# Attention with one query: loads of eight heads at 64 KiB per partition in three buffers, with V loaded one place behind K

## The chip, the cores and the metric

The kernel runs on one NeuronCore of a Trainium2 chip; the other cores of the chip are idle. The metric is the time of one execution on the device in microseconds, lower is better. The span of a profile, from the first to the last instruction, is about 1.7 us shorter than the time of the same execution (before: 1260.5 against 1262.21 us).

## The reference

```python
B, H, Sq, Skv, Dh = 8, 32, 1, 4096, 128        # bfloat16
def reference(q, k, v):
    scale = q.shape[-1] ** -0.5
    scores = jnp.einsum('bhqd,bhkd->bhqk', q, k) * scale
    attn = softmax(scores, axis=-1)
    return jnp.einsum('bhqk,bhkd->bhqd', attn, v)
```

There are 256 heads with one query each. Every K and V element is used once: 536.9 MB must be read, and little is computed with each byte.

## The kernel before

A tile is the K (or V) of G = 4 heads: 128 partitions, 32 of them for each head, C = 128 positions in each partition, 128 values per position, 32 KiB per partition, 4 MiB in one load. Five such buffers are shared by K and V. For each tile VectorE (DVE) multiplies K by the query and adds the upper half of the products to the lower (`product`); TensorE (PE) sums the remaining 64 values with an identity matrix into PSUM (`sum_over_d`); DVE finishes the sums and finds one maximum per head (`weights_of`); ScalarE (ACT) takes the exponentials, one pass per head, into a weights tile `w`; PE multiplies weights and V (`values_of`), and a last small product picks each head's own block (`result_of`). `norm_of` sums the exponentials on PE and takes the reciprocal on DVE: this is the normaliser. The last few positions of the last V are multiplied straight into the result, in small matmuls at the very end (the "late" matmuls).

```python
G = 4
SLOTS = 5
R = 4
LAST = 8
# [cut: constants, pools, the query, product, sum_over_d]

    def weights_of(t):
        # [cut: scores from PSUM, maximum, bias per head]
        w = w_pool.tile([P, C, G], BF16, name="w", tag="w")
        # [cut]
        for g in range(G):
            nc.scalar.activation(
                out=w[:, :, g], in_=sc[:], func=ACT.Exp, bias=bias[:, g : g + 1], scale=scale,
                accum_out=esum[:, t % R, g : g + 1],
            )

    def values_of(t, lo, hi):
        # [cut]
        for c0 in range(lo, hi, CB):                     # CB = 4 positions per matmul
            nc.tensor.matmul(
                avs[t][:], lhsT=w[:, c0 : c0 + CB, :], rhs=vt[:, c0 : c0 + CB, :],
                start=(c0 == 0), stop=(c0 + CB == (C if t < NT - 1 else C - LAST)),
            )

    # [cut]
    for t in range(NT - 1):                              # NT = 64
        if t + 2 < NT:
            load("k", t + 2)
        load("v", t)
        # [cut]
        product(t, 0, C // 2)
        if t > 0:
            weights_of(t - 1)
        product(t, C // 2, C)
        if t > 1:
            values_of(t - 2, 0, C)
            result_of(t - 2)
            # [cut: norm_of]
        sum_over_d(t)
    load("v", NT - 1)
    with tc.manual_schedule():
        product(NT - 1, 0, C // 2)
        weights_of(NT - 2)
        product(NT - 1, C // 2, C)
        values_of(NT - 3, 0, C)
        result_of(NT - 3)
        sum_over_d(NT - 1)
        values_of(NT - 2, 0, C // 2)
        weights_of(NT - 1)
        values_of(NT - 2, C // 2, C)
        result_of(NT - 2)
        norm_of(NQ - 1)
        values_of(NT - 1, 0, C - LAST)
        result_of(NT - 1)
```

## Time and profile before

| | before |
|---|---|
| time, median of 3 | 1262.19 us (1262.17 to 1262.36) |
| span of the profile | 1260.5 us |
| DMA between 20 and 1200 us | share 1.00, 431 GB/s |
| last data packet ends | 1254.4 us |
| from there to the end of the span | 6.1 us |

The page of the profile, in parts: the load queue with bytes and its share of the 16 DMA engines; the chain of work that ended last; the exponentials (count, busy time, mean time of one); and the loads, with their number, size and median time from issue to landing.

```profile
q1 hardware_dynamic: 20160, 536.88, 99.2%
...
DMA 67%; PE 24%; DVE 7%; ACT 1%; issue 0%; SPq 0%; ACTq 0%; DVEq 0%
...
L203 ACT ACTIVATE w<-sc,bias 128x128 bf16<-128x128 f32 x256 | 110.9, 567 | 734.0 <-DVE bias L195 734.0
...
kt<-in_k_dram SPq DMA_DIRECT2D x63, 4096.0 KB, 35.2
vt<-in_v_dram SPq DMA_DIRECT2D x61, 4096.0 KB, 29.6
```

The loads take 99.2% of the DMA engines' time and 67% of the chain, so they are what bounds the kernel. A 4 MiB load needs 9.7 us at 431 GB/s, but 29.6 to 35.2 us pass from its issue to its landing: by these medians two other loads were queued ahead of it, so a buffer that comes free a little late costs nothing.

The windows view of before shows each stretch of time with its length, the busy time and number of instructions of PE, weight loads, DVE, ACT and POOL, the granted TensorE clock (1 is full), the DMA share and the rate.

```profile
core 0: us, PE busy (x) PEld busy (x) DVE busy (x) ACT busy (x) POOL busy (x), PEclk, DMA share, GB/s
20.00:1200.00 1180.00, 795.08 (x3193) 297.45 (x3193) 901.54 (x812) 151.22 (x567) 0.00 (x0) 0.83 1.00 431
...
1245.00:1250.00 5.00, 4.33 (x26) 1.78 (x24) 0.33 (x2) 0.77 (x3) 0.00 (x0) 1.00 0.83 340
1250.00:1255.00 5.00, 5.00 (x25) 2.10 (x24) 0.00 (x0) 0.00 (x0) 0.00 (x0) 1.00 0.31 123
```

The DMA is saturated until about 1245 us and runs out between 1245 and 1255 us. The kernel's end is therefore two things: when the last data land, and how much work is still to be done then.

The timeline of before, cut to the end of the kernel. The columns are start, duration, engine, line, operation, output and inputs, count, and in brackets the idle time before it with what ended it.

```profile
1215.84 0.13 PEld L219 LDWEIGHTS <-w 128*16 128x16 bf16 x1 [0.29 <-issue]
1216.26 0.13 PEld L219 LDWEIGHTS <-w 128*16 128x16 bf16 x1 [0.29 <-issue]
...
1241.44 7.07 PE L219 MATMUL av<-vt,w 128*16 128x512 bf16 x32
...
1243.45 0.58 ACT L203 ACTIVATE w<-sc,bias 128x128 bf16<-128x128 f32 x1 [5.94 <-DVE bias L195]
...
1243.85 0.56 ACT L203 ACTIVATE w<-sc,bias 128x128 bf16<-128x128 f32 x1
...
1249.56 6.63 PE L219 MATMUL av<-vt,w 128*16 128x512 bf16 x30
...
1256.23 0.59 ACT L240 ACTIVATE comb<-av 16x512 bf16<-16x512 f32 x1 [7.09 <-PE av L219]
...
1258.22 0.33 ACTq L265 DMA_DIRECT2D out_dram<-stage  x1
```

Weight loads stand 0.42 us apart at the start of a burst of matmuls, while the 32 and the 30 matmuls (7.07 and 6.63 us) run at 0.22 us each: PE is slow at first and then twice as fast. And the exponentials of 128 columns start 0.40 us apart (0.385 us between the next ones). After the last V matmul the rest (copy, combining, late matmuls, store) takes about 4.3 us.

The length of single DMA packets is in the trace's packet records, not on the page. For the load queue of before (bytes, number, median and mean ns):

```
32768  15872  1216   1219.0
16384    256   611.5  613.3
 8192   1408   313    313.7
    4   2240     9      9.1    (semaphore of each load, one per engine)
```

A straight line through the means of these sizes has about 27 GB/s per engine and a fixed part of about 9 ns per packet.

### The profile page before, as it was taken

To read this page: it belongs to the slowest core of one execution; us is meant where nothing else is said; L and a number is where in the kernel's file an instruction comes from. 1 tells how busy PE (TensorE), PEld (TensorE's weight loads), DVE (VectorE), ACT (ScalarE), POOL (GpSimd) and SP (SyncE) were. 2 spreads that over 40 slices of the span, in tenths; PEclk is the share of its full clock that TensorE was granted. 3 is DMA by queue.
4 is the path that set the end of the run, shared out by engine and by line. 5 is a ranking of instruction groups with operands and counts; after the bars stand their busy time and mean duration, and the time that the engine had idled before them with its cause. 6 is when DMAs were issued, how large, how long until landed. Compare 5 with 4: busy or idle time off the path is not lost.

```text
span 1260.5 us, 8779 instructions
## 1 busy us (share of the span) xinstructions
PE 845.2 (67%) x3430; PEld 317.2 (25%) x3430; DVE 940.4 (75%) x851; ACT 164.3 (13%) x609; POOL 2.9 (0%) x14
## 2 busy tenths in 40 slices
PE   1666766856757667677676675766767667667578
PEld 0222222322222222222232222222222222222223
DVE  5869978687686777877778768677686777876873
ACT  0101111111101111011111110110101101111011
POOL 0000000000000000000000000000000000000000
PEclk9778878888789788887787888888888788887889
DMA  9999999999999999999999999999999999999996
GB/s 400 432 431 431 430 433 430 430 430 430 432 432 430 429 433 432 432 433 431 431 432 433 428 432 432 432 429 430 432 431 430 433 432 432 430 431 431 429 424 287
DMA packets 20569, 537.57 MB, mean 426 GB/s; under 512 B 2592, under 2 KB 2592, under 8 KB 2992
## 3 DMA queue, kind: packets, MB, share of 16 engines
q1 hardware_dynamic: 20160, 536.88, 99.2%
q8 instruction: 27, 0.44, 0.1%
q10 hardware_dynamic: 368, 0.13, 0.0%
q14 instruction: 14, 0.11, 0.0%
HBM read 536.94 MB, written 0.07 MB: 426 GB/s over the span
## 4 chain that ended last, share of the span: by engine, by line
DMA 67%; PE 24%; DVE 7%; ACT 1%; issue 0%; SPq 0%; ACTq 0%; DVEq 0%
DMA vt<-in_v_dram 66%; PE av L219 22%; DVE kt L150 4%; DVE kt L153 2%; PE ps L167 2%; DMA kt<-in_k_dram 1%; ACT w L203 0%; DVE sc L180 0%; PE op L244 0%; ACT comb L240 0%; DVE pmax L184 0%; SPq L124 0%; DVE bias L195 0%; DVE spread L186 0%; DVE nmax L191 0%
## 5 line engine op out<-in xcount | busy, mean ns | idle before, releaser
L219 PE MATMUL av<-vt,w 128*16 128x512 bf16 x2046 | 571.9, 449 | 344.1 <-DMA vt<-in_v_dram 344.1
L150 DVE TENSOR_TENSOR kt<-kt,qb 128x4096 bf16<-128x4096 bf16 x256 | 579.1, 2283 | 214.7 <-DMA kt<-in_k_dram 214.7
L219 PEld LDWEIGHTS <-w 128*16 128x16 bf16 x2046 | 207.6, 102 | 704.3 <-issue 537.3
L153 DVE TENSOR_TENSOR kt<-kt 128x2048 bf16<-128x2048 bf16 x256 | 305.7, 1215 | 0.1
L167 PE MATMUL ps<-kt,ident 128*128 128x512 bf16 x1024 | 253.2, 390 | 32.4 <-DVE kt L153 32.4
L203 ACT ACTIVATE w<-sc,bias 128x128 bf16<-128x128 f32 x256 | 110.9, 567 | 734.0 <-DVE bias L195 734.0
L167 PEld LDWEIGHTS <-ident 128*128 128x128 bf16 x1024 | 90.7, 98 | 161.3 <-issue 61.1
L203 ACT ACTIVATION_READ_ACCUMULATOR w<-sc,bias 128x1 f32 x256 | 64.8, 253 | 0.0
L180 DVE TENSOR_REDUCE sc<-ps 128x128 f32<-128x512 f32 x64 | 43.7, 683 | 24.6 <-PE ps L167 24.6
L240 ACT ACTIVATE comb<-av 16x512 bf16<-16x512 f32 x64 | 37.6, 588 | 167.8 <-PE av L219 132.2
L235 DVE RECIPROCAL rz<-zp 16x1 f32<-16x1 f32 x16 | 2.5, 155 | 66.9 <-PE zp L230 66.9
L141 ACT ACTIVATE qb<-qp 128x512 bf16<-128x512 f32 x16 | 9.6, 597 | 179.6 <-DVE kt L150 174.0
L244 PE MATMUL op<-comb,pick 16*16 16x128 bf16 x256 | 25.0, 217 | 6.4 <-ACT comb L240 6.4
L244 PEld LDWEIGHTS <-pick 16*16 16x16 bf16 x256 | 13.7, 84 | 34.2 <-issue 34.2
L135 PE MATMUL qp<-q_all,ident 16*32 16x512 bf16 x64 | 7.6, 430 | 21.6 <-ACT qb L141 14.9
L184 DVE TENSOR_REDUCE pmax<-sc 128x1 f32<-128x128 f32 x64 | 17.7, 277 | 0.1
L186 DVE TENSOR_SCALAR spread<-zero,pmax 128x32 f32<-128x32 f32 x64 | 14.9, 233 | 0.1
L195 DVE TENSOR_SCALAR bias<-own,nmax 128x4 f32<-128x4 f32 x64 | 14.3, 223 | 0.1
L191 DVE TRANSPOSE_TENSOR_REDUCE nmax<-spread 128x1 f32<-128x32 f32 x64 | 13.0, 202 | 0.1
L135 PEld LDWEIGHTS <-ident 16*32 16x32 bf16 x64 | 1.8, 89 | 28.4 <-issue 26.8
L230 PE MATMUL zp<-ones,esum 128*16 128x1 f32 x32 | 3.1, 166 | 8.1 <-ACT w L203 8.1
L259 ACT ACTIVATE stage<-op,rz 16x128 bf16<-16x128 f32 x16 | 5.7, 358 | 11.3 <-PE op L244 10.3
(21 smaller groups left out, 9.0 us busy)
## 6 DMA issues: line engine op xcount, KB each, us to landing
kt<-in_k_dram SPq DMA_DIRECT2D x63, 4096.0 KB, 35.2
vt<-in_v_dram SPq DMA_DIRECT2D x61, 4096.0 KB, 29.6
vt<-in_v_dram SPq DMA_DIRECT2D x11, 1024.0 KB, 22.3
kt<-in_k_dram SPq DMA_DIRECT2D x2, 2048.0 KB, 33.5
vt<-in_v_dram SPq DMA_DIRECT2D x1, 512.0 KB, 18.5
vt<-in_v_dram SPq DMA_DIRECT2D x2, 256.0 KB, 15.8
q_all<-in_q_dram ACTq DMA_DIRECT2D x1, 64.0 KB, 5.9
out_dram<-stage ACTq DMA_DIRECT2D x3, 16.0 KB, 9.9
```

The lines of the kernel that those rows point to most:

```text
L150: nc.vector.tensor_tensor(out=part, in0=part, in1=qb[:, j : j + 1, :].to_broadcast([P, MC, D]), op=ALU.mult)
L153: nc.vector.tensor_tensor(out=part[:, :, 0 : D // 2], in0=part[:, :, 0 : D // 2], in1=part[:, :, D // 2 : D], op=ALU.add,)
L167: nc.tensor.matmul(ps[:], lhsT=ident[:], rhs=kt[:, u * UC : (u + 1) * UC, s * DS : (s + 1) * DS], start=(s == 0), stop=(s == n - 1),)
L180: nc.vector.tensor_reduce(out=sc[:, u * UC : (u + 1) * UC], in_=ps[:], axis=AX.X, op=ALU.add)
L184: nc.vector.tensor_reduce(out=pmax[:], in_=sc[:], axis=AX.X, op=ALU.max)
L186: nc.vector.tensor_scalar(out=spread[:], in0=zero[:], scalar1=pmax[:, 0:1], scalar2=-scale, op0=ALU.add, op1=ALU.mult,)
L191: nc.vector.tensor_reduce(out=nmax[:], in_=spread[:], axis=AX.X, op=ALU.min, apply_transpose=True)
L195: nc.vector.tensor_scalar(out=bias[:], in0=own[:], scalar1=nmax[:, 0:1], scalar2=None, op0=ALU.add)
L203: nc.scalar.activation(out=w[:, :, g], in_=sc[:], func=ACT.Exp, bias=bias[:, g : g + 1], scale=scale, accum_out=esum[:, t % R, g : g + 1],)
L219: nc.tensor.matmul(avs[t][:], lhsT=w[:, c0 : c0 + CB, :], rhs=vt[:, c0 : c0 + CB, :], start=(c0 == 0), stop=(c0 + CB == (C if t < NT - 1 e ...
L240: nc.scalar.activation(out=comb[:], in_=avs.pop(t)[:], func=ACT.Copy)
L244: nc.tensor.matmul(ops[n][:], lhsT=pick[:, m, r, :], rhs=comb[:, m * D : (m + 1) * D], start=(r == 0 and m == 0), stop=(r == R - 1 and m = ...
```

## The change

The tile doubles to eight heads: 64 KiB per partition, 8 MiB per load, with three buffers in place of five. There are half as many loads and packets of, perhaps, twice the size. With only three buffers, each has to be emptied in time, so the schedule is written out by hand and fine-grained: scores in quarters of a tile, each V loaded one place behind its K, and its matmuls spread over the products of two tiles. The first and last loads are cut, and the last tile's exponentials come in two halves, to shorten both ends.

The diff, cut to its core:

```diff
-G = 4
-SLOTS = 5
-R = 4
+G = 8
+SLOTS = 3
+R = 2
-LAST = 8
+LAST = 16
-    UC = 128
+    UC = 64
[cut: pools, query, constants]
     cuts = {
-        ("k", NT - 1): [C // 2] * 2,
-        ("v", NT - 3): [C // 4] * 4,
+        ("k", 0): [C // 4] * 4,
+        ("k", NT - 4): [C // 2] * 2,
+        ("k", NT - 3): [C // 2] * 2,
+        ("k", NT - 2): [C // 2] * 2,
+        ("k", NT - 1): [C // 4] * 4,
         ("v", NT - 2): [C // 4] * 4,
-        ("v", NT - 1): [C // 4] * 3 + [C // 8, C // 16, LAST],
+        ("v", NT - 1): [C // 8] * 7 + [C // 16, LAST],
     }
[cut: q_prep per tile; sum_over_d and scores_of per quarter]
-        for g in range(G):
-            nc.scalar.activation(
-                out=w[:, :, g], in_=sc[:], func=ACT.Exp, bias=bias[:, g : g + 1], scale=scale,
-                accum_out=esum[:, t % R, g : g + 1],
-            )
+        n = C // 2 if t == NT - 1 else C
+        for c0 in range(0, C, n):
+            if c0 > 0:
+                esum = late
+            for g in range(G):
+                nc.scalar.activation(
+                    out=w[:, c0 : c0 + n, g], in_=sc[:, c0 : c0 + n], func=ACT.Exp,
+                    bias=bias[:, g : g + 1], scale=scale, accum_out=esum[:, t % R, g : g + 1],
+                )
[cut: the loop of before and its end]
+    with tc.manual_schedule():
+        q_prep(0)
+        for t in range(NT):                     # NT is now 32
+            if t + 1 < NT:
+                load("k", t + 1)
+            load("v", t)
+            product(t, 0, Q)                    # Q = C // 4
+            if t > 1:
+                values_of(t - 2, 3 * Q, 3 * Q + Q // 2)
+            sum_over_d(t, 0)
+            if t > 1:
+                values_of(t - 2, 3 * Q + Q // 2, C)
+                copy_of(t - 2)
+            if t + 1 < NT:
+                q_prep(t + 1)
+            product(t, Q, 2 * Q)
+            sum_over_d(t, 1)
+            scores_of(t, 0)
+            if t > 1:
+                if t % R == 1:
+                    norm_of(t // R - 1)
+                result_of(t - 2)
+            if t > 0:
+                values_of(t - 1, 0, Q)
+            product(t, 2 * Q, 3 * Q)
+            sum_over_d(t, 2)
+            scores_of(t, 1)
+            if t > 0:
+                values_of(t - 1, Q, 2 * Q)
+            product(t, 3 * Q, C)
+            sum_over_d(t, 3)
+            scores_of(t, 2)
+            scores_of(t, 3)
+            weights_of(t)
+            if t > 0:
+                values_of(t - 1, 2 * Q, 3 * Q)
+        values_of(NT - 2, 3 * Q, C)
+        copy_of(NT - 2)
+        norm_of(NQ - 1)
+        result_of(NT - 2)
+        values_of(NT - 1, 0, C - LAST)
+        copy_of(NT - 1)
+        result_of(NT - 1)
```

More of the change, by code (lines that the diff above doesn't have):

```diff
@@ L40 @@
     scale = float(D) ** -0.5
-    UC = 128
+    UC = 64
     DS = 512 // UC
     NU = C // UC
-    MC = 32
+    MC = UC
     CB = 4
@@ L47 @@
     NQ = NT // R
-    assert NQ <= P and C % CB == 0
-    q_n = q.rearrange("b h o d -> (b h o d)").rearrange("(n x) -> n x", n=NQ)
+    TB = 32
+    assert NH % P == 0 and P % G == 0 and TB % PH == 0 and C % CB == 0
+    q_n = q.rearrange("b h o d -> (b h o) d").rearrange("(x p) d -> p x d", p=P)
     o_n = out.rearrange("b h o d -> (b h o) d").rearrange("(n u x) d -> n x u d", u=OB, x=RG)
@@ L57 @@
     q_pool = ctx.enter_context(tc.tile_pool(name="q_pool", bufs=2))
-    w_pool = ctx.enter_context(tc.tile_pool(name="w_pool", bufs=3))
-    small = ctx.enter_context(tc.tile_pool(name="small", bufs=4))
-    o_pool = ctx.enter_context(tc.tile_pool(name="o_pool", bufs=2))
-    ps_s = ctx.enter_context(tc.tile_pool(name="ps_s", bufs=2, space=bass.MemoryType.PSUM))
+    w_pool = ctx.enter_context(tc.tile_pool(name="w_pool", bufs=2))
+    sc_pool = ctx.enter_context(tc.tile_pool(name="sc_pool", bufs=1))
+    small = ctx.enter_context(tc.tile_pool(name="small", bufs=2))
+    o_pool = ctx.enter_context(tc.tile_pool(name="o_pool", bufs=1))
+    ps_s = ctx.enter_context(tc.tile_pool(name="ps_s", bufs=3, space=bass.MemoryType.PSUM))
     ps_v = ctx.enter_context(tc.tile_pool(name="ps_v", bufs=2, space=bass.MemoryType.PSUM))
-    ps_o = ctx.enter_context(tc.tile_pool(name="ps_o", bufs=2, space=bass.MemoryType.PSUM))
+    ps_o = ctx.enter_context(tc.tile_pool(name="ps_o", bufs=1, space=bass.MemoryType.PSUM))
     ps_q = ctx.enter_context(tc.tile_pool(name="ps_q", bufs=1, space=bass.MemoryType.PSUM))
     ps_z = ctx.enter_context(tc.tile_pool(name="ps_z", bufs=1, space=bass.MemoryType.PSUM))
-    q_all = consts.tile([NQ, R, G, D], BF16, name="q_all")
-    nc.scalar.dma_start(q_all.rearrange("n r g d -> n (r g d)"), q_n)
+    q_all = consts.tile([P, NH // P, D], BF16, name="q_all")
+    nc.scalar.dma_start(q_all[:], q_n)
     ident = consts.tile([P, P], BF16, name="ident")
@@ L73 @@
         out=ident[:], in_=ident[:], pattern=[[-1, P]], compare_op=ALU.not_equal,
+        fill=1.0, base=0, channel_multiplier=1,
+    )
+    heads = consts.tile([G, G, PH], BF16, name="heads")
+    nc.gpsimd.memset(heads[:], 0.0)
+    nc.gpsimd.affine_select(
+        out=heads[:], in_=heads[:], pattern=[[-1, G], [0, PH]], compare_op=ALU.not_equal,
         fill=1.0, base=0, channel_multiplier=1,
@@ L85 @@
         fill=NEG, base=PH - 1, channel_multiplier=-1,
+    )
+    same = consts.tile([P, TB], F32, name="same")
+    nc.vector.tensor_reduce(
+        out=same[:].rearrange("p (h x) -> p h x", x=PH),
+        in_=own[:].rearrange("p (b h) -> p h b", h=TB // PH)
+        .rearrange("p h (o b) -> p h o b", o=1)
+        .to_broadcast([P, TB // PH, PH, P // TB]),
+        axis=AX.X, op=ALU.max,
     )
@@ L101 @@
     )
-    zero = consts.tile([P, 32], F32, name="zero")
-    nc.vector.memset(zero[:], 0.0)
     ones = consts.tile([P, 1], F32, name="ones")
     nc.vector.memset(ones[:], 1.0)
+    late = consts.tile([P, R, G], F32, name="late")
+    nc.vector.memset(late[:], 0.0)
     w_last = consts.tile([P, LAST, RG], BF16, name="w_last")
@@ L130, in q_prep @@
     def q_prep(t):
-        if t % R == 0:
-            n = t // R
-            qp = ps_q.tile([P, R, D], F32, name="qp", tag="qp")
-            for g in range(G):
-                nc.tensor.matmul(
-                    qp[g * PH : (g + 1) * PH, :, :],
-                    lhsT=ident[0:NQ, n : n + 1].to_broadcast([NQ, PH]),
-                    rhs=q_all[:, :, g, :], start=True, stop=True,
-                )
-            qb = q_pool.tile([P, R, D], BF16, name="qb", tag="qb")
-            nc.scalar.activation(out=qb[:], in_=qp[:], func=ACT.Copy)
-            qbs[n] = qb
+        x, p0 = divmod(t * G, P)
+        qh = ps_q.tile([G, D], F32, name="qh", tag="qp")
+        nc.tensor.matmul(
+            qh[:], lhsT=ident[:, p0 : p0 + G], rhs=q_all[:, x, :], start=True, stop=True
+        )
+        qg = q_pool.tile([G, D], BF16, name="qg", tag="qg")
+        nc.scalar.activation(out=qg[:], in_=qh[:], func=ACT.Copy)
+        qp = ps_q.tile([P, D], F32, name="qp", tag="qp")
+        nc.tensor.matmul(qp[:], lhsT=heads[:].rearrange("g h x -> g (h x)"), rhs=qg[:], start=True, stop=True)
+        qb = q_pool.tile([P, 1, D], BF16, name="qb", tag="qb")
+        nc.scalar.activation(out=qb[:, 0, :], in_=qp[:], func=ACT.Copy)
+        qbs[t] = qb
     def product(t, lo, hi):
         kt = loads["k", t]
-        qb = qbs[t // R]
-        j = t % R
+        qb = qbs[t]
         for c0 in range(lo, hi, MC):
@@ L150, in product @@
             nc.vector.tensor_tensor(
-                out=part, in0=part, in1=qb[:, j : j + 1, :].to_broadcast([P, MC, D]), op=ALU.mult
+                out=part, in0=part, in1=qb[:].to_broadcast([P, MC, D]), op=ALU.mult
             )
@@ L158, with sum_over_d, scores_of @@
     sums = {}
-    def sum_over_d(t):
-        kt = loads.pop(("k", t))
-        sums[t] = []
-        for u in range(NU):
-            ps = ps_s.tile([P, UC, DS], F32, name="ps", tag="ps")
-            n = D // 2 // DS
-            for s in range(n):
-                nc.tensor.matmul(
-                    ps[:], lhsT=ident[:],
-                    rhs=kt[:, u * UC : (u + 1) * UC, s * DS : (s + 1) * DS],
-                    start=(s == 0), stop=(s == n - 1),
-                )
-            sums[t].append(ps)
+    def sum_over_d(t, u):
+        kt = loads["k", t]
+        ps = ps_s.tile([P, UC, DS], F32, name="ps", tag="ps")
+        n = D // 2 // DS
+        for s in range(n):
+            nc.tensor.matmul(
+                ps[:], lhsT=ident[:],
+                rhs=kt[:, u * UC : (u + 1) * UC, s * DS : (s + 1) * DS],
+                start=(s == 0), stop=(s == n - 1),
+            )
+        sums[t, u] = ps
+    scs = {}
+    def scores_of(t, u):
+        if u == 0:
+            scs[t] = sc_pool.tile([P, C], F32, name="sc", tag="sc")
+        nc.vector.tensor_reduce(
+            out=scs[t][:, u * UC : (u + 1) * UC], in_=sums.pop((t, u))[:], axis=AX.X, op=ALU.add
+        )
     ws = {}
@@ L177, in weights_of @@
     def weights_of(t):
-        sc = small.tile([P, C], F32, name="sc", tag="sc")
-        for u, ps in enumerate(sums.pop(t)):
-            nc.vector.tensor_reduce(
-                out=sc[:, u * UC : (u + 1) * UC], in_=ps[:], axis=AX.X, op=ALU.add
-            )
+        sc = scs.pop(t)
         pmax = small.tile([P, 1], F32, name="pmax", tag="pmax")
         nc.vector.tensor_reduce(out=pmax[:], in_=sc[:], axis=AX.X, op=ALU.max)
-        spread = small.tile([P, 32], F32, name="spread", tag="spread")
+        spread = small.tile([P, TB], F32, name="spread", tag="spread")
         nc.vector.tensor_scalar(
-            out=spread[:], in0=zero[:], scalar1=pmax[:, 0:1], scalar2=-scale,
+            out=spread[:], in0=same[:], scalar1=pmax[:, 0:1], scalar2=-scale,
             op0=ALU.add, op1=ALU.mult,
@@ L201, in weights_of @@
         esum = esums[t // R]
-        for g in range(G):
-            nc.scalar.activation(
-                out=w[:, :, g], in_=sc[:], func=ACT.Exp, bias=bias[:, g : g + 1], scale=scale,
-                accum_out=esum[:, t % R, g : g + 1],
-            )
+        n = C // 2 if t == NT - 1 else C
[6 more added lines that the diff above has]
+                    bias=bias[:, g : g + 1], scale=scale, accum_out=esum[:, t % R, g : g + 1],
+                )
         ws[t] = w
@@ L229, in norm_of, with copy_of @@
         zp = ps_z.tile([RG, 1], F32, name="zp", tag="zp")
-        nc.tensor.matmul(
-            zp[:], lhsT=esums.pop(n).rearrange("p r g -> p (r g)"), rhs=ones[:],
-            start=True, stop=True,
-        )
+        parts = [esums.pop(n)] + ([late] if n == NQ - 1 else [])
+        for i, e in enumerate(parts):
+            nc.tensor.matmul(
+                zp[:], lhsT=e.rearrange("p r g -> p (r g)"), rhs=ones[:],
+                start=(i == 0), stop=(i == len(parts) - 1),
+            )
         rzs[n] = small.tile([RG, 1], F32, name="rz", tag="rz")
         nc.vector.reciprocal(out=rzs[n][:], in_=zp[:])
+    combs = {}
+    def copy_of(t):
+        comb = small.tile([CB * G, CB * D], BF16, name="comb", tag="comb")
+        nc.scalar.activation(out=comb[:], in_=avs.pop(t)[:], func=ACT.Copy)
+        combs[t] = comb
     def result_of(t):
         n, r = divmod(t, R)
-        comb = small.tile([CB * G, CB * D], BF16, name="comb", tag="comb")
-        nc.scalar.activation(out=comb[:], in_=avs.pop(t)[:], func=ACT.Copy)
+        comb = combs.pop(t)
         if r == 0:
@@ L265, in result_of @@
             nc.scalar.dma_start(o_n[s, :, lo : u + 1, :], stages[s][:, lo : u + 1, :])
-    q_prep(0)
+    Q = C // 4
     load("k", 0)
-    load("k", 1)
-    for t in range(NT - 1):
-        if t + 2 < NT:
-            load("k", t + 2)
-        load("v", t)
-        if t + 2 < NT:
-            q_prep(t + 2)
-        product(t, 0, C // 2)
-        if t > 0:
-            weights_of(t - 1)
-        product(t, C // 2, C)
-        if t > 1:
-            values_of(t - 2, 0, C)
-            result_of(t - 2)
-            if (t - 2) % R == R - 2:
-                norm_of((t - 2) // R)
-        sum_over_d(t)
-    load("v", NT - 1)
-    with tc.manual_schedule():
-        product(NT - 1, 0, C // 2)
-        weights_of(NT - 2)
-        product(NT - 1, C // 2, C)
-        values_of(NT - 3, 0, C)
-        result_of(NT - 3)
-        sum_over_d(NT - 1)
-        values_of(NT - 2, 0, C // 2)
-        weights_of(NT - 1)
-        values_of(NT - 2, C // 2, C)
+    with tc.manual_schedule():
+        q_prep(0)
[36 more added lines that the diff above has]
+        norm_of(NQ - 1)
         result_of(NT - 2)
-        norm_of(NQ - 1)
         values_of(NT - 1, 0, C - LAST)
+        copy_of(NT - 1)
         result_of(NT - 1)
```

## The prediction

> **What bounds the kernel now.** The loads. The windows view shows DMA share 1.00 and 431-432 GB/s from 20 to 1230 us; DVE is busy 75% and PE 67% of the span (page, part 1). The DMA issue list shows 29.6-35.2 us from issue to landing for a 4 MiB load that takes 9.7 us to move: two loads always wait in the queue. The Trainium skill ("DMA: Bandwidth & Descriptors", Where 436 GB/s comes from) states a ceiling of 435 GB/s; 536.9 MB at that is an estimated 1234 us, so at most 28 us can be won. The trace's packet records put the last landing near 1253 us; the kernel ends 7 us later.
>
> **Steady part.** Bytes, multiplies, adds and matmul counts stay.
> - Transfer: the packet records show 32 KiB packets of 1218 ns, 16 KiB 613, 8 KiB 314: about 8.6 ns fixed each, plus one semaphore packet per load and engine (about 14 ns with its gap). If a 64 KiB row goes as one packet, 1249 us of transfer lose about 5 us; if cut in two, 1 us.
> - DVE (timeline pitches: 4096-element multiply 2.20 us, add 1.14): doubled ops about 4.34 and 2.20, a quarter tile 6.5, a tile 26.2; scores 4 x 0.6, the maximum chain 1.4: 30 of the 38.9 us per K+V pair, plus waits for PE.
> - PE: the timeline shows matmuls 427 ns apart for the first 5-6 us of a burst, then about 220 (the skill, "TensorE: Matmul & The Clock Gate", Part 1, has the same two rates). A pair needs 96: 21 us warm, 41 us cold.
> - Slots: each load must be consumed within two load times (38.9 us) of landing. V(t-1) lands 19.4 us after K(t); then values 6.2, sums 1.8, values 3.5, sums 1.8: K(t) is free about 33 us after landing. V(t-1) is finished after the next tile's first sums, also about 33 us. About 6 us spare: the DMA stays saturated, issue to landing near 25 us.
>
> **The ends.** Start: DVE begins near 9-10 us instead of 14, but loads set the pace: no gain. End (E = last landing): V29 lands at E-58; PE must take its first quarter before the sums of K30, so the weights of 30 are done only at E-43, although K30 came in halves. K31 then costs DVE 34 us: maximum chain done E-9, sixteen exponentials at 0.385 us until E-3; the normaliser and the copy of V30's result stand before V31 in order, so V31's 60 matmuls (13.2 us) run from E-2 to E+11.5; combining, 16 late matmuls and the store take 5 us: the end is E+16, against E+7 now. So 9 us of tail are lost, 1-5 us of transfer won.
>
> **Predicted time: 1266 us, 8 in 10 within 1254 to 1275.** Faster by over 2%: 0.01. Within 2%: 0.93. Slower by over 2%: 0.06.
>
> **What would show it right or wrong.** Steady DMA 432-434 GB/s, share 1.00; packets of 65536 or 32768 bytes and their duration; issue to landing near 25 us; DVE idle a few us before each tile's first product, and DVE scores waiting for PE sums that wait for V; V31's matmuls back to back without waiting for DMA, ending some 11 us after the last landing.
>
> **What would make it wrong.** PE staying cold in short bursts, so that buffers free too late and the DMA gaps every pair (1 us per pair is 32 us: the slower case). Slower HBM access for rows 64 KiB apart. A tail in which V31 keeps up with its landings: then 1256-1258. Skew of the 16 DMA engines that three buffers no longer absorb.

One correction to its text: counted from the first instruction, as everything else here is, the last packet of before ends at 1254.4 us (not "near 1253"), and the span ends 6.1 us later (not 7).

## The result, and the profile after

The changed kernel takes 1270.36 us (median of 4, 1270.05 to 1272.47), before 1262.28 us in the same rounds: ratio 1.0067, 95% interval 1.005 to 1.0085. A ratio here is the mean time of one kernel's fast runs over that of the other's of the same rounds, so it is not quite the ratio of the medians. The profiled execution was the slowest of the four (1272.47 us). An unaltered copy, run later as a control, took 1269.99 us, and its profile has a span of 1266.9 us; where the two profiles differ, both are given.

| | before | after | control |
|---|---|---|---|
| span of the profile, us | 1260.5 | 1270.8 | 1266.9 |
| last data packet ends, us | 1254.4 | 1249.9 | 1248.7 |
| from there to the end, us | 6.1 | 20.9 | 18.2 |

So the loads end 4.5 to 5.7 us earlier, and the work behind them grows by 12.0 to 14.8 us (from the unrounded times). The page of after, the same parts as before:

```profile
q1 hardware_dynamic: 12096, 536.88, 98.0%
...
DMA 61%; DVE 20%; PE 17%; ACT 1%; issue 0%; DVEq 0%
...
L230 ACT ACTIVATE w<-sc,bias 128x256 bf16<-128x256 f32 (+1 forms) x264 | 301.2, 1557 | 624.8 <-DVE bias L218 624.8
...
vt<-in_v_dram SPq DMA_DIRECT2D x30, 26.1
kt<-in_k_dram SPq DMA_DIRECT2D x27, 26.2
```

The loads still take 98% of the DMA engines' time, but only 61% of the chain: DVE now has 20% of it. Issue to landing is 26.1 to 26.2 us for an 8 MiB load that moves in 19.4 us: one load waits in the queue, with some 7 us to spare, and that is enough. ACT's exponentials are about as many (264 against 256), nearly all on twice the columns, but their busy time went from 110.9 to 301.2 us, to more than twice.

The windows view of after, for the same stretches and one more:

```profile
20.00:1200.00 1180.00, 783.59 (x3065) 303.34 (x3065) 930.72 (x504) 318.10 (x585) 0.00 (x0) 0.83 1.00 432
...
1245.00:1250.00 5.00, 0.67 (x6) 0.26 (x5) 0.18 (x1) 5.00 (x19) 0.00 (x0) 0.82 0.51 208
1250.00:1255.00 5.00, 4.79 (x16) 1.85 (x15) 0.17 (x2) 0.21 (x1) 0.00 (x0) 0.50 0.00 0
1255.00:1260.00 5.00, 5.00 (x24) 2.26 (x23) 0.00 (x0) 0.00 (x0) 0.00 (x0) 0.99 0.00 0
```

Over the middle the rate is 432 GB/s at share 1.00, against 431. At the end the picture differs: the DMA falls silent before 1250 us, PE is nearly idle from 1245 to 1250 us, and then works for another 16 us, the first 5 of them at half clock (0.50).

The timeline of after, from the landing of V29 (the V of the third tile from the end) to the end:

```profile
1191.36 6.40 PE L246 MATMUL av<-vt,w 128*32 128x512 bf16 x16 [9.09 <-DMA vt<-in_v_dram]
...
1199.63 0.69 DVE L197 TENSOR_REDUCE sc<-ps 128x64 f32<-128x512 f32 x1 [5.10 <-PE ps L185]
...
1206.72 0.23 DVE L218 TENSOR_SCALAR bias<-own,nmax 128x8 f32<-128x8 f32 x1
...
1240.12 0.23 DVE L218 TENSOR_SCALAR bias<-own,nmax 128x8 f32<-128x8 f32 x1
1240.38 0.86 ACT L230 ACTIVATE w<-sc,bias 128x128 bf16<-128x128 f32 x1 [17.34 <-DVE bias L218]
...
1240.78 1.04 ACT L230 ACTIVATE w<-sc,bias 128x128 bf16<-128x128 f32 x1
...
1249.31 0.89 ACT L270 ACTIVATE comb<-av 32x512 bf16<-32x512 f32 x1
...
1249.84 0.21 PE L259 MATMUL zp<-ones,late 128*16 128x1 f32 x2 [4.33 <-ACT w L230]
...
1250.77 15.23 PE L246 MATMUL av<-vt,w 128*32 128x512 bf16 x60
...
1268.47 0.34 ACTq L300 DMA_DIRECT2D out_dram<-stage  x1
```

Read it from the top. PE waits 9.09 us for V29; DVE waits 5.10 us for the sums that stand behind V29's matmuls; the bias of tile 30, the end of its maximum chain, comes at 1206.72 us, that of tile 31 at 1240.12 us. The last tile's sixteen exponentials of 128 columns then start 0.57 us apart; ACT turns to its next work at 1249.3 us, and the last of them ends at 1249.8 us. The normaliser waits for them, and V31's 60 matmuls start behind it at 1250.77 us, when all of V31 has landed, and take 15.23 us.

The packet records of after show packets of 65536 bytes: 7296 of them, median 2420 ns, mean 2427 ns, against two of 32768 bytes at 1219 ns in before. A row of 64 KiB does go as one packet record.

### The profile page after: what moved, and what is told of

The parts are those of the page before. It is cut to its first block, busy times and chain, and to the rows that moved or that the text cites. A ratio compares the mean times of both kernels' runs of the same rounds, so it can differ in the third digit from the quotient of the medians.

```text
span 1270.8 us, 8147 instructions
## 1 busy us (share of the span) xinstructions
PE 837.4 (66%) x3310; PEld 326.2 (26%) x3310; DVE 968.7 (76%) x532; ACT 341.1 (27%) x641; POOL 2.8 (0%) x16
## 4 chain that ended last, share of the span: by engine, by line
DMA 61%; DVE 20%; PE 17%; ACT 1%; issue 0%; DVEq 0%
DMA kt<-in_k_dram 54%; DVE kt L170 13%; PE ps L185 9%; PE av L246 8%; DVE kt L173 7%; DMA vt<-in_v_dram 6%; DMA q_all<-in_q_dram 1%; ACT w L230 1%; DVE sc L197 0%; DVEq L170 0%; PE qh L154 0%; ACT comb L270 0%; PE op L285 0%; PE op L279 0%; DVE pmax L207 0%
## 5 line engine op out<-in xcount | busy, mean ns | idle before, releaser
L170 DVE TENSOR_TENSOR kt<-kt,qb 128x8192 bf16<-128x8192 bf16 x128 | 565.1, 4415 | 136.9 <-DMA kt<-in_k_dram 124.7
L246 PE MATMUL av<-vt,w 128*32 128x512 bf16 x2044 | 526.9, 417 | 112.6 <-DMA vt<-in_v_dram 112.6
L185 PE MATMUL ps<-kt,ident 128*128 128x512 bf16 x1024 | 298.6, 444 | 274.1 <-DVE kt L173 273.9
L230 ACT ACTIVATE w<-sc,bias 128x256 bf16<-128x256 f32 (+1 forms) x264 | 301.2, 1557 | 624.8 <-DVE bias L218 624.8
L246 PEld LDWEIGHTS <-w 128*32 128x32 bf16 x2044 | 205.7, 104 | 428.8 <-issue 250.3
L173 DVE TENSOR_TENSOR kt<-kt 128x4096 bf16<-128x4096 bf16 x128 | 293.4, 2292 | 4.4
L185 PEld LDWEIGHTS <-ident 128*128 128x128 bf16 x1024 | 105.3, 108 | 466.3 <-issue 348.8
L197 DVE TENSOR_REDUCE sc<-ps 128x64 f32<-128x512 f32 x128 | 87.6, 685 | 97.4 <-PE ps L185 97.4
L230 ACT ACTIVATION_READ_ACCUMULATOR w<-sc,bias 128x1 f32 x264 | 130.8, 496 | 0.0
L270 ACT ACTIVATE comb<-av 32x512 bf16<-32x512 f32 x32 | 19.1, 596 | 233.2 <-PE qh L154 155.8
L154 PE MATMUL qh<-q_all,ident 128*8 128x128 bf16 x32 | 7.2, 224 | 13.9 <-DMA q_all<-in_q_dram 13.9
L207 DVE TENSOR_REDUCE pmax<-sc 128x1 f32<-128x256 f32 x32 | 13.4, 420 | 1.1
## 6 DMA issues: line engine op xcount, KB each, us to landing
kt<-in_k_dram SPq DMA_DIRECT2D x8, 2048.0 KB, 19.4
vt<-in_v_dram SPq DMA_DIRECT2D x30, 26.1
kt<-in_k_dram SPq DMA_DIRECT2D x27, 26.2
```

Of the source, the lines that this page charges most:

```text
L170: nc.vector.tensor_tensor(out=part, in0=part, in1=qb[:].to_broadcast([P, MC, D]), op=ALU.mult)
L173: nc.vector.tensor_tensor(out=part[:, :, 0 : D // 2], in0=part[:, :, 0 : D // 2], in1=part[:, :, D // 2 : D], op=ALU.add,)
L185: nc.tensor.matmul(ps[:], lhsT=ident[:], rhs=kt[:, u * UC : (u + 1) * UC, s * DS : (s + 1) * DS], start=(s == 0), stop=(s == n - 1),)
L197: nc.vector.tensor_reduce(out=scs[t][:, u * UC : (u + 1) * UC], in_=sums.pop((t, u))[:], axis=AX.X, op=ALU.add)
L207: nc.vector.tensor_reduce(out=pmax[:], in_=sc[:], axis=AX.X, op=ALU.max)
L230: nc.scalar.activation(out=w[:, c0 : c0 + n, g], in_=sc[:, c0 : c0 + n], func=ACT.Exp, bias=bias[:, g : g + 1], scale=scale, accum_out=esu ...
```

## The experiments

Each edit is made to the changed kernel. The excess is the median minus the median of before in the same rounds; the last column is the excess minus the control's, rounded only at the end. The runs were made on three chips (c_after, e_split, e_v29half and e_early on one, e_stride8, e_stride2, e_warm and e_qsync on a second, e_sumsfirst and e_best on a third), which is why the excess and not the time is compared. The control ran on the first chip only.

| run | median us | ratio to before (95%) | excess us | against control us |
|---|---|---|---|---|
| c_after (control) | 1269.99 | 1.0059 (1.0046 to 1.0072) | +7.6 | |
| e_split | 1273.73 | 1.0089 (1.0075 to 1.0103) | +11.4 | +3.7 |
| e_v29half | 1263.45 | 1.0010 (0.9996 to 1.0023) | +1.1 | -6.5 |
| e_early | 1263.69 | 1.0010 (0.9997 to 1.0024) | +1.3 | -6.3 |
| e_stride8 | 1265.40 | 1.0028 (1.0014 to 1.0042) | +3.3 | -4.3 |
| e_stride2 | 1265.52 | 1.0033 (1.0019 to 1.0047) | +3.4 | -4.2 |
| e_warm | 1268.88 | 1.0051 (1.0038 to 1.0064) | +6.8 | -0.8 |
| e_qsync | 1269.68 | 1.0060 (1.0047 to 1.0074) | +7.6 | 0.0 |
| e_sumsfirst | 1266.05 | 1.0035 (1.0020 to 1.0050) | +4.1 | -3.6 |
| e_best | 1256.60 | 0.9957 (0.9944 to 0.9969) | -5.4 | -13.0 |

All ten gave the right result.

### Control: is the loss in the tail or spread over the run?

The kernel is the changed one, without an edit.

> Control: the changed kernel, unaltered, on the same chip as the next runs. Theory T (the loss lies in the tail): ratio to before 1.006 to 1.008; last landing near 1249 us against 1253 us in before, and the last instruction some 20 to 22 us after it. Rival R (three buffers cost the DMA some gap in every pair, so the loss is spread over the run): last landing not earlier than in before.

Ratio 1.0059, last packet at 1248.7 us, the end 18.2 us after it. The rival is refuted: with three buffers the loads end earlier than with five, not later. The theory's "20 to 22 us" was too high for this execution: its chain ran 2.7 us closer to the last packet than in the profiled run of after (the table under "Why the prediction was right or wrong", and the account below it).

### Packet size

```diff
+    for t_ in range(NT - 4):
+        if t_ > 0:
+            cuts["k", t_] = [C // 2] * 2
+        cuts["v", t_] = [C // 2] * 2
```

> All loads of K1 to K27 and V0 to V27 are issued as two loads of 32 KiB per partition, the last four pairs and everything else as they are. Theory P (a 64 KiB packet saves fixed time: 8 x 2420 + 14 ns against 16 x 1216 + 28 ns per engine and load): 55 loads x 0.09 to 0.11 us = 5 to 6 us slower than the control, last landing later by the same, tail after it unchanged. Rival Q (the earlier last landing comes from the start or from which engine is slowest, not from packet size): within 1 us of the control.

It was 3.7 us slower than the control, with the last packet at 1253.2 us, 4.5 us later, and the end 19.2 us after that. The packet records have 14848 packets of 32768 bytes with a mean of 1218.3 ns. From the means, one load costs an engine 16 x 1218.3 + 28 = 19521 ns in two pieces and 8 x 2427 + 14 = 19430 ns in one; times 55 loads that is 5.0 us. The measured 3.7 to 4.5 us is a little under the expected 5 to 6 us, but the rival's "within 1 us" is excluded. The larger packet is what the change won.

### Where the tail comes from: V29

```diff
+        ("v", NT - 3): [C // 2] * 2,
         ("v", NT - 2): [C // 4] * 4,
```

> Only V29 is loaded in halves. Theory G (the weights of K30 wait until all of V29 has landed, because V29's first matmuls stand before K30's sums in PE order): its first half lands 9.7 us earlier, the maximum chains of tiles 30 and 31 come about 8 us earlier, and the kernel is 6 to 8 us faster than the control. Rival H (the DVE work on K30 and K31 alone sets when tile 31's weights are ready): no change, within 1 us.

It was 6.5 us faster than the control. The timeline of this run: the bias of tile 30, that of tile 31, and V31's matmuls.

```profile
1197.25 0.23 DVE L219 TENSOR_SCALAR bias<-own,nmax 128x8 f32<-128x8 f32 x1
...
1230.65 0.23 DVE L219 TENSOR_SCALAR bias<-own,nmax 128x8 f32<-128x8 f32 x1
...
1241.30 15.76 PE L247 MATMUL av<-vt,w 128*32 128x512 bf16 x60
```

The bias of tile 30 comes at 1197.25 us instead of 1206.72 us (in the control at 1203.61 us), that of tile 31 at 1230.65 us instead of 1240.12 us (1237.00 us). Cutting one load in two, with no other edit, moved DVE's whole chain forward by 6.4 to 9.5 us. Six other runs leave V29 and its order as in the control and load it at the same time (after, e_early, e_stride8, e_stride2, e_warm, e_qsync): with the control their bias of tile 30 comes at 1203.6 to 1206.7 us, so 1197.25 us is outside what differs from one execution to the next. The rival, that DVE's own work sets the time, is refuted. V31's matmuls, now started before all of V31 has landed, still take 15.76 us.

The same cause was then tested without touching the load, by the order on PE alone:

```diff
-            if t > 0:
+            if t > 0 and t != NT - 2:
                 values_of(t - 1, 0, Q)
[cut]
-            if t > 0:
+            if t > 0 and t != NT - 2:
                 values_of(t - 1, Q, 2 * Q)
             product(t, 3 * Q, C)
             sum_over_d(t, 3)
+            if t == NT - 2:
+                values_of(t - 1, 0, 2 * Q)
```

> V29 is loaded whole, as in the changed kernel; only in tile 30 the third and fourth quarter's sums stand before V29's first two quarters of matmuls on PE. Theory G (the wait for V29 in PE order holds up the weights of K30): the maximum chain of tile 30 comes about 8 us earlier and the kernel is 6 to 8 us faster than the changed one, as with V29 in halves. Rival: halving V29 helped by the finer load itself (an earlier free buffer or an earlier issue), not by the order: under 1 us here.

It was 3.6 us faster than the control: the cause is confirmed (1199.40 us for the bias of tile 30 is again outside 1203.6 to 1206.7 us), the size was expected too high. The timeline of this run shows why: the last sums of tile 30 and V29's matmuls on PE, the bias of tile 30, and DVE's wait for the normaliser of tile 31.

```profile
1194.09 3.57 PE L185 MATMUL ps<-kt,ident 128*128 128x512 bf16 x8 [3.95 <-DVE kt L173]
...
1197.59 13.42 PE L246 MATMUL av<-vt,w 128*32 128x512 bf16 x56
...
1199.40 0.23 DVE L218 TENSOR_SCALAR bias<-own,nmax 128x8 f32<-128x8 f32 x1
...
1216.68 0.15 DVE L264 RECIPROCAL rz<-zp 16x1 f32<-16x1 f32 x1 [3.04 <-PE zp L259]
```

The bias of tile 30 came at 1199.40 us, 4.2 us before the control's. It could not come much sooner: without V29's matmuls in between PE had been idle, and the last eight sums ran at the slow rate, 3.57 us. Then the V29 matmuls that had been put back ran together with those that follow them, in one piece of 56, 13.42 us long, in front of tile 31's first sums, and DVE waited 3.04 us at the normaliser behind them (1.51 us in the control). Part of the gain went into these two new waits.

### The order at the end

```diff
         copy_of(NT - 2)
+        values_of(NT - 1, 0, C // 2)
         norm_of(NQ - 1)
         result_of(NT - 2)
-        values_of(NT - 1, 0, C - LAST)
+        values_of(NT - 1, C // 2, C - LAST)
```

> The first half of V31's matmuls is put before the normaliser and V30's result in PE order, nothing else. Theory O (V31 starts late only because of that order, its first-half weights being ready 4.5 us before the last): V31's matmuls start about 5 us earlier and at full rate, and the kernel is 6 to 8 us faster than the control. Rival S (V31's matmuls wait for all sixteen exponentials themselves, whatever the order): under 1 us of change.

It was 6.3 us faster than the control. In the timeline of this run, the first 32 of V31's matmuls start at 1242.87 us, before the exponentials are finished (the copy behind them starts at 1246.91 us), and the other 28 follow the normaliser:

```profile
1242.87 7.08 PE L246 MATMUL av<-vt,w 128*32 128x512 bf16 x32
...
1246.91 0.90 ACT L270 ACTIVATE comb<-av 32x512 bf16<-32x512 f32 x1
...
1249.84 0.19 PE L259 MATMUL zp<-ones,late 128*16 128x1 f32 x2
...
1250.27 6.21 PE L246 MATMUL av<-vt,w 128*32 128x512 bf16 x28
```

The 60 take 7.08 + 6.21 = 13.3 us in two pieces, all at the full rate. The halves of the exponentials, which the change had introduced, were useless in its own order, because the normaliser, which needs both halves, stood in front.

### The exponentials

Within each group of four positions the weights are stored as (half of the heads, position, head in the half). A matmul still reads 32 neighbouring columns; `pick` is permuted to match.

```diff
-        w = w_pool.tile([P, C, G], BF16, name="w", tag="w")
+        w = w_pool.tile([P, C // CB, 2, CB, 4], BF16, name="w", tag="w")
[cut]
-                    out=w[:, c0 : c0 + n, g], in_=sc[:, c0 : c0 + n], func=ACT.Exp,
+                    out=w[:, c0 // CB : (c0 + n) // CB, g // 4, :, g % 4],
+                    in_=sc[:, c0 : c0 + n].rearrange("p (b c) -> p b c", c=CB), func=ACT.Exp,
[cut: pick, w_last, lhsT to match]
```

> The weights tile is laid out so that one head's exponentials are written 8 bytes apart (as in before) and not 16 bytes apart; matmul columns stay 32 in a row, the picking matrix is permuted to match. Theory W (the exponentials take 0.57 us each for 128 columns, against 0.385 us in before, because of the step of the write): starts 0.38 to 0.40 us apart in the last tile, the sixteen done about 3 us earlier, the kernel 3 to 5 us faster than the changed kernel (5 if PE then no longer idles long enough to slow down). Rival X (they are slower because eight heads or the weight loads on PE share the memory): still 0.57 us apart.

It was 4.3 us faster than the control. The timeline of this run, two exponentials of the last tile and V31's matmuls:

```profile
1237.98 0.57 ACT L224 ACTIVATE w<-sc,bias 128x128 bf16<-128x128 f32 x1 [17.34 <-DVE bias L212]
...
1238.38 0.55 ACT L224 ACTIVATE w<-sc,bias 128x128 bf16<-128x128 f32 x1
...
1245.09 13.12 PE L246 MATMUL av<-vt,w 128*32 128x512 bf16 x60
```

They start 0.40 us apart (0.385 us between the later ones), the sixteen take 6.2 us instead of 8.9 us, PE's wait gets short enough that its clock stays up, and V31's 60 matmuls take 13.12 us. In the second form the four positions of one head are neighbours, 2 bytes apart:

```diff
+        w = w_pool.tile([P, C // CB, G, CB], BF16, name="w", tag="w")
```

> The same with four neighbouring columns of one head 2 bytes apart, then a step of 64 bytes. Theory W: at most the 0.385 us of the 8-byte step, perhaps less; kernel 3 to 5 us faster than the changed one. Rival X: still 0.57 us.

It gave the same 0.385 us for 128 columns and the same time, 4.2 us under the control. The 256-column exponentials in the middle of the run separate the three layouts: in the timelines they start 1.14 us apart with the 16-byte step, 0.64 us with the 8-byte step, 0.49 us with runs of four. Both readings say that the step of the write was the cost; the rival is refuted. Only the last tile's sixteen are on the critical path, so the large saving elsewhere is worth nothing in time.

### PE's clock

```diff
         copy_of(NT - 2)
+        busy = ps_s.tile([P, 512], F32, name="busy", tag="ps")
+        for _ in range(20):
+            nc.tensor.matmul(
+                busy[:], lhsT=ident[:],
+                rhs=loads["k", NT - 1][:, 0:4, :].rearrange("p c d -> p (c d)"),
+                start=True, stop=True,
+            )
         norm_of(NQ - 1)
```

> Twenty matmuls whose result nobody reads are put on PE where it waits for the last exponentials (about 4.4 us at full rate, in a wait of 5.3 us). Theory C (the idle wait lets the clock fall, and the first ten of V31's 60 matmuls run at half rate): the 60 take 13.2 us instead of 15.2, kernel 2 us faster than the changed one. Rival: V31's matmuls are slow at first for another reason (data or weights just landed): still 15.2 us.

The timeline of this run, the twenty idle matmuls and V31's 60:

```profile
1244.58 4.49 PE L344 MATMUL busy<-kt,ident 128*128 128x512 bf16 x20
...
1249.86 13.12 PE L246 MATMUL av<-vt,w 128*32 128x512 bf16 x60
```

The 60 take 13.12 us, as expected, where they take 15.23 us in after and 14.49 us in the control. So the slow start was the clock, fallen in the wait. The time as a whole is only 0.8 us under the control, which the runs (1267.6 to 1269.5 against 1268.2 to 1271.0 us) do not clearly separate; for the mechanism the trace decides, for its worth in time the answer stays between nothing and 2 us. (After is the fairer trace to compare: in both the bias of tile 31 comes 9.75 us before the last packet, and V31's matmuls end 13.9 us behind it here, 16.1 us in after.)

### The start

```diff
-    nc.scalar.dma_start(q_all[:], q_n)
+    nc.sync.dma_start(q_all[:], q_n)
```

> The queries are loaded ahead of K0 on the same queue instead of beside it on another queue. Theory A (256-byte packets of the query queue take turns with 16 KiB packets of the K queue, so the queries land at 13 us): queries land before 4 us, the first DVE product starts near 7 us instead of 15 us, and the kernel's time stays within 1 us because the loads set the pace. Rival: the start is on the critical path, and the kernel gets several us faster.

The timeline of this run, the first query matmul and the first product:

```profile
2.69 0.27 PE L154 MATMUL qh<-q_all,ident 128*8 128x128 bf16 x1 [2.69 <-DMA q_all<-in_q_dram]
...
9.05 4.42 DVE L170 TENSOR_TENSOR kt<-kt,qb 128x8192 bf16<-128x8192 bf16 x1 [6.21 <-DMA kt<-in_k_dram]
```

The queries are there at 2.69 us instead of 13.86 us, DVE starts at 9.05 us (the first quarter of K0 lands at 9.0 us) instead of 15.08 us, and the time is that of the control. The start is off the critical path, as predicted; that DVE would begin at 9 to 10 us in the changed kernel was wrong.

### All together

The cut of V29, the order at the end, the 8-byte step and the queries first, as above.

> V29 in halves, half of V31 before the normaliser, weights written 8 bytes apart, queries ahead of K0, all together. The gains overlap, since V31 cannot end before it lands: last landing near 1249 us, then about 5 us for the last four matmuls, combining, the late matmuls and the store: 1254 us in the trace, 1256 us timed, ratio to before 0.995. Rival (the three each remove the same wait, so nothing is added): 1262 us.

It takes 1256.60 us (1256.37 to 1256.70), 5.4 us less than before in the same rounds, ratio 0.9957 (0.9944 to 0.9969): by a small margin, but clear of noise, the fastest of all. Its timeline at the end:

```profile
1228.94 13.99 PE L247 MATMUL av<-vt,w 128*32 128x512 bf16 x64
...
1247.34 2.75 PE L247 MATMUL av<-vt,w 128*32 128x512 bf16 x12 [0.46 <-DMA vt<-in_v_dram]
...
1250.13 0.59 ACT L271 ACTIVATE comb<-av 32x512 bf16<-32x512 f32 x1 [12.35 <-PE av L247]
...
1252.56 0.34 ACTq L301 DMA_DIRECT2D out_dram<-stage  x1
```

PE works on V30 and the first half of V31 without a pause (64 matmuls from 1228.94 us), then waits only for data, and the last V matmuls end at 1250.1 us, with the last packet at 1249.4 us. What remains is the 4.8 us of combining and storing.

## Why the prediction was right or wrong

The verdict, within 2%, and the range (1254 to 1275 us) held. The point, 1266 us, was 4 us low: about 4 us of loss were forecast (9 lost, 5 won), and 8 us were measured. The range is wide enough to hold the time of before as well, so that it held says little; the single steps say more.

- **Loads bound the kernel and stay saturated with three buffers**: right. Share 1.00 and 432 GB/s in the middle (432 to 434 predicted), issue to landing 26 us (25 predicted), DVE waits of 4.8 us before a tile's first product (124.7 us in 26), score reductions waiting for PE (97.4 us).
- **"1-5 us of transfer won"**: right at the upper branch. Packets of 65536 bytes, last packet 4.5 to 5.7 us earlier, and cutting the packets in two gave 3.7 to 4.5 us back.
- **"no gain" at the start**: right, shown by e_qsync. The time of DVE's first product was wrong: 15.08 us, not 9 to 10, because the queries landed late.
- **"9 us of tail are lost"**: right in mechanism, too small: 12.0 us in the control, 14.8 us in the profiled run. Of the gap, 0.9 us lies in before, whose end is E+6.1 and not E+7; the rest is in the steps. Against the last packet E:

| step | predicted | after | control |
|---|---|---|---|
| V29's first matmul | E-58 | E-58.5 | E-59.0 |
| weights of 30 can start | E-43 | E-42.9 | E-44.9 |
| maximum chain of 31 done | E-9 | E-9.5 | E-11.5 |
| sixteen exponentials done | E-3 | E-0.1 | E-2.1 |
| V31's matmuls start | E-2 | E+0.9 | E-1.1 |
| V31's matmuls end | E+11.5 | E+16.1 | E+13.4 |
| end of the span | E+16 | E+20.9 | E+18.2 |

In the second row the prediction says "done", but its own sum (34 us of DVE from there to E-9) is that of DVE's chain; the exponentials of tile 30 themselves ended at E-33.4 in after. The chain up to the maximum is as predicted or earlier; e_v29half and e_sumsfirst show its first cause and e_early its last. Two terms of the sum were mis-sized. The step "sixteen exponentials at 0.385 us" took that duration from before, where the writes of a head stand 8 bytes apart; eight heads make the step 16 bytes and the duration 0.57 us, 8.9 us instead of 6.2 us. The Trainium skill would have warned of it ("SBUF — State Buffer", Door 1, the note on cachelines: lines of 16 bytes, with at least two hits per line for full bandwidth; a step of 16 bytes has one), and the prediction does not draw on it. The runs show that the step costs the time; that the lines are the reason is the page's account, which they fit. The term "V31's 60 matmuls (13.2 us)" took the full rate for granted: the longer exponentials made PE wait, its clock fell, and the 60 took 14.5 to 15.2 us. The skill ("TensorE: Matmul & The Clock Gate", Part 1) puts the fall after an idle window of about 3.4 us; the wait here was 4.33 us after the last small matmul, and the clock view reads 0.50 behind it, so the trace agrees. Together these are 2.7 + 1.3 to 2.0 = 4.0 to 4.7 us; in the control a maximum chain 2.5 us earlier than predicted hides part of it. The last part, 5 us from V31's last matmul to the end, was right (4.7 to 4.8 us).

After and the control are one kernel, and yet their ends differ by 2.7 us. The timeline of the control, V29's first sixteen matmuls and V31's 60, to be held against the same lines of after:

```profile
1189.70 4.94 PE L246 MATMUL av<-vt,w 128*32 128x512 bf16 x16 [8.47 <-DMA vt<-in_v_dram]
...
1247.64 14.49 PE L246 MATMUL av<-vt,w 128*32 128x512 bf16 x60
```

V29's first matmul lies 0.5 us earlier against the last packet, its first sixteen take 4.94 us and not 6.40 (mean granted clock 0.72 and 0.56), and V31's 60 take 14.49 us and not 15.23: 0.5 + 1.5 + 0.7 = 2.7 us, so most of the difference is PE's clock. In the clock records of the traces every stretch of full or half clock lasts a multiple of 3.41 us (all 1470 records of the twelve traces, but for the last of each, which the end cuts off). So how much of a burst runs slowly depends on where in this step it begins: V31's matmuls met a half-clock stretch of 6.8 us in after (1248.2 to 1255.1 us) and one of 3.4 us in the control (1247.0 to 1250.5 us). What sets the 0.5 us in V29's landing stays open.

## What to carry to other kernels

When a kernel is already at its transfer rate, a change of the load size can win only the fixed time per packet (here about 5 us of 1250), and its larger grain can lose more at the end than that: follow the last few loads by hand, from each landing to the last instruction, in the order in which each engine's queue holds the work. An early-arriving operand or an early half of the weights is worth nothing if something that needs the late half stands in front of it in the same queue. Before a duration is carried over from another shape, check that the step of its writes stays the same.

## What the Trainium skill lacked or had wrong

- "SBUF — State Buffer" (Door 1, the note on cachelines) gives no duration for a step of the writes, "ScalarE: Activation LUTs" (What ACT_TABLE_LOAD costs) gives an activation's duration by its number of columns alone, and the note's "8 bf16" as the stride that is still free cannot be read as a step of 8 elements. Here an exponential of 256 columns with bf16 output starts every 1.14 us with a 16-byte step, 0.64 us with an 8-byte step and 0.49 us in runs of four neighbours; with 128 columns it is 0.57, 0.385 and 0.385 us. With two hits per line (8 bytes) the longer one was thus still not at its best.
- "DMA: Bandwidth & Descriptors" (Bandwidth) gives about 10.5 ns per packet for a 4 KB transfer and (Why small descriptors are slow) a fixed overhead of about 3 cycles per packet, but no duration for large packets. Here the records show 65536 bytes in 2420 ns and 32768 in 1216 ns (medians), about 9 ns fixed from a line through the sizes of before; a 64 KiB row is one packet record, while the page speaks of packets of 4096 bytes as preferred (SWDGE vs HWDGE vs iDMA).
- "DMA: Bandwidth & Descriptors" (Queues, rings and completion order, Arbitration) says that engines take turns between queues packet by packet. The runs agree, with one 256-byte row in each turn (on each engine the sixteen rows start some 0.6 us apart, the time of a 16 KiB packet), and add what it costs: 64 KiB of queries in 256-byte rows beside K in 16 KiB packets landed at 13.8 us, ahead of K on the same queue before 2.7 us.
- "TensorE: Matmul & The Clock Gate" (Part 1): the two rates agree; matmuls of 512 columns stood 0.427 us apart after a wait of 4.33 us and 0.22 us apart later, and twenty matmuls with no use kept the clock up. But the idle window of about 3.4 us is no safe bound: in the control a wait of 3.02 us (before 1226.12 us) was followed by half clock from 1226.6 us and eight sums of 3.17 us, while the same wait in after (before 1229.23 us) was followed by eight of 1.89 us.
